# Where the sums for seven half products are made: from the second layer's first block into its second

## The chip, the cores and the metric

The kernel runs on one core of a Trainium2 chip. That core has TensorE (PE: matmuls, with its weight loads listed as PEld), VectorE (DVE), ScalarE (ACT), GpSimd (POOL) and SyncE (SP), which here only starts DMAs. The engines run beside each other; each takes its own instructions strictly in the order of the program and waits on semaphores for the others. The metric is the time of one execution on the device, in microseconds (us); lower is better.

## The reference

Three stages, one after another, all in float32: a linear attention with decay, then a layer with a rational function, then a layer with a cosine. The change lies in the last one.

```python
# attention: state = alpha[t] * state + outer(k[t], v[t]); y[t] = q[t] @ state     (4 x 8 heads, 768 steps, 48 wide)
# first layer, 3072 tokens, 384 -> 2048 -> 384
h = x @ w_in
P = a[0] + a[1] * h + a[2] * h**2 + a[3] * h**3
Q = 1.0 + abs(b[0]) * abs(h) + abs(b[1]) * h**2
x = (P / (Q + 1e-06)) @ w_out
# second layer, the same sizes, weights of its own
h = x @ w_in
out = (h * cos(h)) @ w_out
```

## The kernel before

**Tiles.** Tokens are columns: 3072 tokens are six blocks of 512 (`NC` = 6, `TB` = 512; `HT` = 256 is half a block). The hidden width 2048 is 16 chunks `f` of 128 (`NF`), the model width 384 is three of 128 (`NK`). A step `n` is one chunk of one block; `layers(n)` (line 797 on) issues one step, and `where(n)` tells layer `m`, block `blk` and chunk `f`. In the second layer (m = 1, n from 96 on) f runs fastest, then the block.

**Precision.** A float32 product is made of three matmuls in the type fp32r: each operand is split into a rounded part ("hi") and the rest ("lo"), and hi x hi, hi x lo and lo x hi are added up (`PASSES`). So a plain step has nine matmuls of 128x512 for h (`gemm1`, L640) and nine for the output (`gemm2`, L656). `gemm2` of a step is issued some steps later, by `lag`: 4 steps for a plain chunk, 5 for one by seven.

**Between the products** (`cosine`): L78 (ACT) and L79 (DVE) reduce the angle, L742 (ACT) takes the sine, L744 (DVE) makes g = h cos h, L686 (ACT) rounds it to hi, and L691 (POOL) makes its lo. hi and lo have three buffers each, g four, z three.

**Weights of the second layer.** They arrive as 64-bit words and are converted by hand, one weight at a time (`tick`, three operations a step here): L67 and L68 on ACT, L72 and L73 on DVE. In the next step `w_hi` rounds (L187, ACT) and `w_lo` makes the rest (L196, POOL). The second layer's output weights are converted during the layer's first block, each about one step before `gemm2` reads it; the last one is done in the second block's third step. Their raw words pass through two buffers named raw, which `seven_out0` also uses for its q.

**Seven half products.** From the second block on (`by_seven`), two neighbouring chunks (a pair, j = f // 2) are multiplied by a scheme that replaces eight products of half a block by seven, at the price of sums. `seven(n, 0)` and `seven(n, 1)` each write the one bank r0 (L566); ACT copies it out at L602 and L608; POOL combines at L603, L614 and L616; DVE adds to h at L625. `seven(n, 2)` makes what is left of both chunks. The scheme needs sums of the weights, once for each pair (`weights_sums(j)`: DVE L516 twice and L520 to L523, ACT L525 twice, POOL L526 twice), and sums of the columns of x, once for each block (`x_sums0`: DVE L533, L537, L538; `x_sums1`: ACT L557 and DVE L558, three of each). `weights_sums` writes one of its results over the first 128 columns of the pair's odd weight, which a plain product of that chunk still needs (for the last pair a tile of its own takes it).

**What sets the order.** The order is written out by hand in `layers`: `gemm1`, `cosine`, `w_hi`, the split of the next block's x (`x_hi`, L785, ACT), `gemm2`, `seven(n, 1)`, `weights_sums`, `x_sums0`, the next block's x loads (f = 8), `x_lo` (L789, DVE, f = 11 to 13), `x_sums1`, then the fetch of weights, `tick` and `w_lo`. In the first block of the second layer `weights_sums` runs in each of the steps f = 8 to 15, one pair a step; `x_sums0` runs at f = 10 and `x_sums1` at f = 14, for the block to come.

Of the kernel before, what the change touches and what calls it, by code (L numbers as in the profile page):

```python
# [10 lines left out]
F32R = mybir.dt.float32r  # L11
# [3 lines left out]
ALU = mybir.AluOpType  # L15
# [3 lines left out]
NC, C = 6, 128  # L19
HP = 4  # L20
NF = DFF // 128
NK = DM // 128
TB = B * C
# [16 lines left out]
def attn_then_two_moe(ctx, tc, kqT, aT, vP, w1i, w1o, ma, mb, w2i, w2o, out):  # L40
    nc = tc.nc
# [40 lines left out]
    const = main.enter_context(tc.tile_pool(name="const", bufs=1))  # L82
# [8 lines left out]
    def temp(tag, dtype=F32, shape=(128, TB)):  # L91

        bufs = {"z": 3, "ah": 2, "g": 4, "hi": 3, "lo": 3}[tag]
        return el.tile(list(shape), dtype, tag=tag, name=tag, bufs=bufs)
# [369 lines left out]
    def where(n):  # L464
        m, r = divmod(n, N1)
        if n < 2 * H1:
            return 0, *divmod(n, H1)
        if n < 2 * NF:
            blk, f = divmod(n - 2 * H1, NF - H1)
            return 0, blk, H1 + f  # L470
        return m, *divmod(r, NF)
# [8 lines left out]
    HT = TB // 2  # L480
    PASSES = ((0, 0), (0, 1), (1, 0))
    s_in = {}
    x_t = {}
    held = {}

    def by_seven(n):

        m, blk, f = where(n)
        return m == 1 and 0 < blk and (blk < NC - 1 or f < NF - 2)

    def lag(n):

# [6 lines left out]

    def weights_sums(j):  # L500

        if j == 0:
            held["kq"] = const.tile([128, 5 * 2 * HP * C], F32R, tag="kq", name="s_in")
            held["s1"] = [const.tile([128, 128], F32R, tag=f"s{i}", name=f"s1_{i}") for i in range(2)]
        if j < 6:
            flat = held["kq"][:, 2 * DM * j:2 * DM * (j + 1)].rearrange("p (a b c) -> p a b c", a=2, b=3)
            s = [flat[:, i] for i in range(2)]
        else:
            s = [
                const.tile([128, 3, 128], F32R, tag=f"v{2 * (j - 6) + i}", name=f"s_in{j}{i}") for i in range(2)  # L510
            ]
        first = held["s1"] if j == NF // 2 - 1 else [ws[0][2 * j + 1][:, i, 0:128] for i in range(2)]
        a = temp("z", shape=(128, 4, 128))
        for i in range(2):
            w = ws[0][2 * j + i].bitcast(F32)
            nc.vector.tensor_tensor(  # L516
                out=a[:, 2 * i:2 * i + 2].rearrange("p a b -> p (a b)"), in0=w[:, 0, 0:256], in1=w[:, 1, 0:256], op=ALU.add
            )
        t = temp("g", shape=(128, 4, 128))
        nc.vector.tensor_tensor(out=t[:, 0], in0=a[:, 2], in1=a[:, 3], op=ALU.add)  # L520
        nc.vector.tensor_tensor(out=t[:, 1], in0=t[:, 0], in1=a[:, 0], op=ALU.subtract)
        nc.vector.tensor_tensor(out=t[:, 2], in0=a[:, 0], in1=a[:, 2], op=ALU.subtract)
        nc.vector.tensor_tensor(out=t[:, 3], in0=a[:, 1], in1=t[:, 1], op=ALU.subtract)  # L523
        for hi, lo, of in ((first[0], first[1], t[:, 0]), (s[0], s[1], t[:, 1:])):
            nc.scalar.activation(out=hi, in_=of, func=AF.Copy)  # L525
            nc.gpsimd.tensor_tensor(out=lo, in0=of, in1=hi.bitcast(F32), op=ALU.subtract)  # L526
        s_in[j] = [[first[i]] + [s[i][:, k] for k in range(3)] for i in range(2)]

    def x_sums0(blk):

        raw = xt[1, blk][:, 1].bitcast(F32)
        t = [in_p.tile([128, TB], F32, tag="p", name="t") for _ in range(2)]
        nc.vector.tensor_tensor(  # L533
            out=t[0].rearrange("p (a b) -> p a b", a=2), in0=raw[:, 0:2, HT:],
            in1=raw[:, 0].rearrange("p (a b) -> p a b", a=2), op=ALU.subtract,
        )
        nc.vector.tensor_tensor(out=t[1][:, :HT], in0=raw[:, 1, HT:], in1=t[0][:, :HT], op=ALU.subtract)  # L537
        nc.vector.tensor_tensor(out=t[1][:, HT:], in0=raw[:, 1, :HT], in1=t[1][:, :HT], op=ALU.subtract)  # L538
        held["t"] = t

    def x_sums1(blk):

        t = held.pop("t")
        tag, words = (("st", 4 * DM), ("a", 3 * HP * (C + 1)))[blk % 2]
        to = const.tile([128, words], F32R, tag=tag, name=f"x_t{blk}")[:, :6 * HT].rearrange(
            "p (a b c) -> p a b c", a=2, b=3
        )
        if blk < NC - 1:
            first = [xt[1, blk][:, i, 0, HT:] for i in range(2)]
        else:  # L550
            first = [held["kq"][:, 12 * DM + HT * i:12 * DM + HT * (i + 1)] for i in range(2)]
        x_t[blk] = [[first[i]] + [to[:, i, k] for k in range(3)] for i in range(2)]
        for hi, lo, of in (
            (first[0], first[1], t[0][:, :HT]), (to[:, 0, 0], to[:, 1, 0], t[0][:, HT:]),
            (to[:, 0, 1:], to[:, 1, 1:], t[1].rearrange("p (a b) -> p a b", a=2)),
        ):
            nc.scalar.activation(out=hi, in_=of, func=AF.Copy)  # L557
            nc.vector.tensor_tensor(out=lo, in0=of, in1=hi.bitcast(F32), op=ALU.subtract)  # L558
# [85 lines left out]
    def gemm2(n):  # L644
        m, blk, f = where(n)
        d = T.pop(n)
        assert m or (0, 1, f) in ready
        first = f == 0 or in_parts(m, blk) and f == H1
        last = f == NF - 1 or in_parts(m, blk) and f == H1 - 1
        for k in range(NK):  # L650
            if first:
                acc_out()
                acc[k] = ps_acc.tile([128, TB], F32, tag=f"acc{k}", name=f"acc{k}")
            ks = slice(k * 128, (k + 1) * 128)
            for i, (w, g) in enumerate(((0, "hi"), (0, "lo"), (1, "hi"))):
                nc.tensor.matmul(  # L656
                    acc[k], ws[1][f][:, w, ks], d[g], start=first and i == 0, stop=last and i == 2
                )
            if last:
                outs.append((m, blk, f, k))  # L660
# [117 lines left out]

    def x_cols(m, blk, kk):

        return slice(0, HT if m and 0 < blk < NC - 1 and kk == 0 else TB)

    def x_hi(m, blk, kk):
        x, cs = xt[m, blk], x_cols(m, blk, kk)
# [16 lines left out]
    def all_ok1():  # L801
        cnt = bank("r1", (1, 2 * NU))
        nc.tensor.matmul(cnt, ones, ok.rearrange("p a b -> p (a b)"), start=True, stop=True)
        tot = const.tile([1, 1], F32, name="tot")
        nc.vector.tensor_reduce(tot, cnt, mybir.AxisListType.X, ALU.add)
        nc.vector.tensor_scalar(bad, tot, 128.0 * 2 * NU - 0.5, None, ALU.is_lt)


    def layers(n):
        slot[0] = n + LEAD  # L810
        if n == N1 + 4:
            gemm2(N1 - 1)
            done[0] += 1
        if n < 2 * N1:
            gemm1(n)
        if n == NF:
            all_ok0()
        if n == NF + 2:
            all_ok1()
        m, r = divmod(n, N1)  # L820
        blk, f = divmod(r, NF)
        nxt = (m, blk + 1) if blk + 1 < NC else (m + 1, 0)
        at, load = f - 11, f == 8
        if n < NF:
            nxt, at, load = (0, 1), n - 5, n == 3
        elif n < 2 * NF:
            at, load = f - 12, f == 10
        split = 0 <= at < NK and n < 2 * N1 and nxt[0] < 2
        rational(n)
        cosine(n)  # L830
        w_hi()
        if split:
            x_hi(*nxt, at)
        second(n)
        if n < 2 * N1 and by_seven(n) and n % 2 == 0:
            seven(n, 1)
            seven_out1(n)
        if m == 1 and blk == 0 and f >= NF // 2:
            weights_sums(f - NF // 2)
        if m == 1 and nxt[0] == 1 and f == 10:  # L840
            x_sums0(nxt[1])
        if n < 2 * N1 and nxt[0] < 2 and load:
            for kk in range(NK):
                x_load(*nxt, kk)
        if split:
            x_lo(*nxt, at)
        if m == 1 and nxt[0] == 1 and f == 14:
            x_sums1(nxt[1])
        i = n - (N1 - NF)
        if n < 2 * NF:  # L850
            if n > 1:
                w_fetch(2 * NF)
                tick(1 if n > 2 else 0, 1)
        elif n < N1 - NF:
            w_fetch(3 * NF + NO)
            if not split:
                tick(1, 1)
        elif n < N1:
            w_fetch(4 * NF)
            if i > 3:  # L860
                tick(1, 1)
        else:
            w_fetch(4 * NF)
            tick(3 if n > N1 + 3 else 1, 1)
        if 0 <= i < NF:
            w_load(i)
        if 0 <= i - 6 < NO:
            w_load(NF + i - 6)
        w_lo([nc.gpsimd])
# [7 lines left out]
    with tc.manual_schedule():  # L877
# [16 lines left out]
        for n in range(-3, NU + 1):  # L894
# [21 lines left out]
            kk = (n - 12) // 2 if n in (12, 14, 16) else None  # L916
# [201 lines left out]
```

## Time and profile before

| | us |
|---|---|
| median of 3 runs (lowest to highest) | 963.41 (962.22 to 965.50) |
| the profiled execution | 964.45 |
| its span, first to last instruction | 962.7 |
| PE busy | 910.3 (95%) |
| DVE busy | 745.5 (77%) |
| ACT busy | 699.6 (73%) |
| POOL busy | 732.0 (76%) |

The rows below come from that one execution; times in them are us from the start of its span. The page splits the span into 40 slices of 24.07 us, with a digit for the busy share of each engine in tenths (9 is 90% or more). A busy share says nothing of who waits for whom: that is in the timeline of an engine, where a bracket behind a row gives how long the engine was idle before it and whose end released it, and in the chain of waits, which follows the work that ended last back from instruction to instruction. PEclk is the granted clock of TensorE, 1.00 being its upper level of 2.4 GHz.

### The profile page before, as it was taken

The numbers are of one execution on the slowest core, as the hardware profiler recorded it, in microseconds if no ns is written. First come the engines' busy times: TensorE is split into PE (matmuls) and PEld (weight loads), VectorE is DVE, ScalarE is ACT, GpSimd is POOL, SyncE is SP. The second block draws the span as 40 slices with busy tenths as digits, with TensorE's granted clock in tenths as the row PEclk, the third lists the DMA queues.
The fourth block names the chain that finished last, engine by engine and source line by source line (L and its number), as shares of the span: only waits on it lengthen the run. The fifth ranks groups of instructions, "written<-read, shape, count | busy, mean of one in ns | idle before, by whom it ended". The sixth has DMA issues, their size and how long they took to land.

```text
span 962.7 us, 15405 instructions
## 1 busy us (share of the span) xinstructions
PE 910.3 (95%) x5327; PEld 751.1 (78%) x5327; DVE 745.5 (77%) x1226; ACT 699.6 (73%) x1280; POOL 732.0 (76%) x693
## 2 busy tenths in 40 slices
PE   7797899999999999999999996699999999999996
PEld 6676777778888888888888874578888888888885
DVE  8988879999999989989799578656647658466451
ACT  6899987879878888788788766566666666666662
POOL 5898998989889888989799555566666666666662
PEclk9999999999999999999999999799999999999999
DMA  8999831101122131141364231120010020200001
GB/s 276 323 313 327 285 116 33 33 17 34 66 82 83 50 115 34 65 132 34 115 205 140 82 115 49 34 83 1 1 66 1 1 66 1 66 1 1 33 1 37
DMA packets 47030, 84.69 MB, mean 88 GB/s; under 512 B 5504, under 2 KB 22144, under 8 KB 46944
## 3 DMA queue, kind: packets, MB, share of 16 engines
q1 hardware_dynamic: 46944, 83.62, 26.5%
q8 instruction: 44, 0.72, 0.3%
q14 instruction: 42, 0.34, 0.1%
HBM read 63.15 MB, written 20.45 MB: 87 GB/s over the span
## 4 chain that ended last, share of the span: by engine, by line
PE 71%; DVE 10%; DMA 7%; ACT 6%; issue 3%; POOL 2%; SPq 1%; DVEq 0%; ACTq 0%; POOLq 0%
PE acc L656 36%; PE b L640 19%; PE r L566 8%; PE b L566 8%; DMA spare<-w1i 2%; DMA x<-x0d 2%; DMA a<-aT 2%; DVE z L516 1%; DMA x0d<-g 1%; DVE g L744 1%; DVE st L72 1%; ACT st L67 1%; ACT hi L686 1%; DVE g L722 1%; POOL w L196 1%
## 5 line engine op out<-in xcount | busy, mean ns | idle before, releaser
L656 PE MATMUL acc<-hi,w 128*128 128x512 f32 x1152 | 394.1, 397 | 19.3 <-POOL w L196 18.2
L691 POOL TENSOR_TENSOR lo<-g,hi 128x512 fp32r<-128x512 f32 x192 | 256.9, 1338 | 98.3 <-ACT hi L686 91.9
L656 PEld LDWEIGHTS acc<-hi,w 128*128 128x128 f32 x1152 | 216.5, 189 | 70.5 <-POOL w L196 21.9
L640 PE MATMUL b<-x,w 128*128 128x512 f32 x1026 | 261.3, 399 | 0.7 <-DVE g L709 0.6
L640 PEld LDWEIGHTS b<-x,w 128*128 128x128 f32 x1026 | 194.3, 190 | 49.8 <-DVE g L709 2.1
L656 PE MATMUL acc<-lo,w 128*128 128x512 f32 x576 | 228.5, 397 | 0.0
L686 ACT ACTIVATE hi<-g 128x512 fp32r<-128x512 f32 x192 | 121.4, 632 | 93.8 <-DVE g L722 51.8
L717 POOL TENSOR_TENSOR z<-z,ah 128x512 f32<-128x512 f32 x96 | 127.3, 1326 | 8.0
L656 PEld LDWEIGHTS acc<-lo,w 128*128 128x128 f32 x576 | 108.5, 188 | 22.9
L744 DVE TENSOR_TENSOR g<-ah,b 128x512 f32<-128x512 f32 x76 | 51.8, 682 | 71.8 <-ACT ah L742 71.8
L79 DVE SCALAR_TENSOR_TENSOR ah<-z,b 128x512 f32<-128x512 int32 x76 | 52.0, 685 | 46.9 <-ACT z L78 46.8
L718 DVE TENSOR_TENSOR g<-g,b 128x512 f32<-128x512 f32 x96 | 65.3, 680 | 24.8 <-ACT g L715 24.2
L716 POOL TENSOR_SCALAR z<-ah,cq 128x512 f32<-128x512 f32 x96 | 75.3, 785 | 1.0 <-ACT ah L714 0.9
L715 ACT ACTIVATE g<-b,cq 128x512 f32<-128x512 f32 x96 | 74.6, 777 | 0.0
L722 DVE SCALAR_TENSOR_TENSOR g<-g,cq,r 128x512 f32<-128x512 f32 x96 | 70.9, 738 | 0.1
L709 DVE SCALAR_TENSOR_TENSOR g<-g,cq,b 128x512 f32<-128x512 f32 x96 | 70.7, 736 | 0.0
L603 POOL TENSOR_TENSOR q<-q 128x256 f32<-128x256 f32 x39 | 28.8, 738 | 53.2 <-ACT q L602 53.2
L742 ACT ACTIVATE ah<-ah,half_pi 128x512 f32<-128x512 f32 x96 | 68.8, 717 | 0.2 <-DVE ah L79 0.2
L726 ACT ACTIVATE r<-z,lnb 128x512 f32<-128x512 f32 x96 | 66.7, 695 | 1.8 <-POOL z L717 1.6
L711 DVE SCALAR_TENSOR_TENSOR r<-z,r 128x512 f32<-128x512 f32 x96 | 65.6, 684 | 0.0
L706 DVE SCALAR_TENSOR_TENSOR z<-z,r 128x512 f32<-128x512 f32 x96 | 65.0, 677 | 0.0
L566 PE MATMUL b<-x,w 128*128 128x256 f32 (+1 forms) x291 | 64.3, 351 | 0.0
(154 smaller groups left out, 1646.5 us busy)
## 6 DMA issues: line engine op xcount, KB each, us to landing
kq<-kqT SPq DMA_DIRECT2D x24, 512.0 KB, 5.4
raw<-w2i SPq DMA_DIRECT2D x16, 384.0 KB, 3.0
w<-wd SPq DMA_DIRECT2D x16, 384.0 KB, 3.0
raw<-w2o SPq DMA_DIRECT2D x16, 384.0 KB, 3.0
v<-vP SPq DMA_DIRECT2D x24, 192.0 KB, 5.0
x<-x0d SPq DMA_DIRECT2D x18, 256.0 KB, 3.5
x1d<-o SPq DMA_DIRECT2D x18, 256.0 KB, 2.1
x<-x1d SPq DMA_DIRECT2D x18, 256.0 KB, 3.6
```

Of the source, the lines that this page charges most:

```text
L566: nc.tensor.matmul(out[:, cs], a[w], b[xx], start=first, stop=True, skip_group_check=True)
L640: nc.tensor.matmul(h, ws[0][f][:, w, ks], x[:, xx, kk, :], start=i == 0, stop=i == 8)
L656: nc.tensor.matmul(acc[k], ws[1][f][:, w, ks], d[g], start=first and i == 0, stop=last and i == 2)
L686: nc.scalar.activation(out=t["hi"], in_=t["g"], func=AF.Copy)
L691: eng.tensor_tensor(out=t["lo"], in0=t["g"], in1=t["hi"].bitcast(F32), op=ALU.subtract)
L709: nc.vector.scalar_tensor_tensor(g, g, cq[:, 3:4], two["h"], ALU.add, ALU.mult)
L715: nc.scalar.activation(out=g, in_=h, func=AF.Identity, scale=cq[:, 5:6], bias=cq[:, 4:5])
L716: nc.gpsimd.tensor_scalar(zz, ah, cq[:, 1:2], cq[:, 0:1], ALU.mult, ALU.add)
L717: nc.gpsimd.tensor_tensor(out=zz, in0=zz, in1=ah, op=ALU.mult)
L722: nc.vector.scalar_tensor_tensor(g, g, cq[:, 2:3], r, ALU.add, ALU.mult)
L726: nc.scalar.activation(out=r, in_=two["z"], func=AF.Ln, scale=LN_S, bias=lnb)
L742: nc.scalar.activation(out=t["r"], in_=t["r"], func=AF.Sin, bias=half_pi)
```

## The change

- The first two pairs of the second layer's second block (blk = 1, f = 0 to 3) become plain steps; `by_seven` takes them out.
- `weights_sums` no longer runs in block 0 (f = 8 to 15). It runs in block 1, at odd f: at f = 1 for pair 2, at f = 3 for pair 3, and so on to pair 7 at f = 11, then pairs 0 and 1 at f = 13 and 15 for the blocks after it.
- For block 1, `x_sums0` (still at block 0's f = 10) runs on POOL instead of DVE, and `x_sums1` runs at block 1's f = 0 instead of block 0's f = 14. As block 1's first chunks are plain, its x is split over the whole block's width, and its first sum goes into the tile kq, as the last block's does.

```diff
--- before.py
+++ after.py
@@ -486,7 +486,7 @@
     def by_seven(n):
 
         m, blk, f = where(n)
-        return m == 1 and 0 < blk and (blk < NC - 1 or f < NF - 2)
+        return m == 1 and 0 < blk and (blk > 1 or f >= 4) and (blk < NC - 1 or f < NF - 2)
 
     def lag(n):
 
@@ -499,8 +499,7 @@
 
     def weights_sums(j):
 
-        if j == 0:
-            held["kq"] = const.tile([128, 5 * 2 * HP * C], F32R, tag="kq", name="s_in")
+        if j == 2:
             held["s1"] = [const.tile([128, 128], F32R, tag=f"s{i}", name=f"s1_{i}") for i in range(2)]
         if j < 6:
             flat = held["kq"][:, 2 * DM * j:2 * DM * (j + 1)].rearrange("p (a b c) -> p a b c", a=2, b=3)
@@ -530,22 +529,25 @@
 
         raw = xt[1, blk][:, 1].bitcast(F32)
         t = [in_p.tile([128, TB], F32, tag="p", name="t") for _ in range(2)]
-        nc.vector.tensor_tensor(
+        eng = nc.gpsimd if blk == 1 else nc.vector
+        eng.tensor_tensor(
             out=t[0].rearrange("p (a b) -> p a b", a=2), in0=raw[:, 0:2, HT:],
             in1=raw[:, 0].rearrange("p (a b) -> p a b", a=2), op=ALU.subtract,
         )
-        nc.vector.tensor_tensor(out=t[1][:, :HT], in0=raw[:, 1, HT:], in1=t[0][:, :HT], op=ALU.subtract)
-        nc.vector.tensor_tensor(out=t[1][:, HT:], in0=raw[:, 1, :HT], in1=t[1][:, :HT], op=ALU.subtract)
+        eng.tensor_tensor(out=t[1][:, :HT], in0=raw[:, 1, HT:], in1=t[0][:, :HT], op=ALU.subtract)
+        eng.tensor_tensor(out=t[1][:, HT:], in0=raw[:, 1, :HT], in1=t[1][:, :HT], op=ALU.subtract)
         held["t"] = t
 
     def x_sums1(blk):
 
         t = held.pop("t")
+        if blk == 1:
+            held["kq"] = const.tile([128, 5 * 2 * HP * C], F32R, tag="kq", name="s_in")
         tag, words = (("st", 4 * DM), ("a", 3 * HP * (C + 1)))[blk % 2]
         to = const.tile([128, words], F32R, tag=tag, name=f"x_t{blk}")[:, :6 * HT].rearrange(
             "p (a b c) -> p a b c", a=2, b=3
         )
-        if blk < NC - 1:
+        if 1 < blk < NC - 1:
             first = [xt[1, blk][:, i, 0, HT:] for i in range(2)]
         else:
             first = [held["kq"][:, 12 * DM + HT * i:12 * DM + HT * (i + 1)] for i in range(2)]
@@ -778,7 +780,7 @@
 
     def x_cols(m, blk, kk):
 
-        return slice(0, HT if m and 0 < blk < NC - 1 and kk == 0 else TB)
+        return slice(0, HT if m and 1 < blk < NC - 1 and kk == 0 else TB)
 
     def x_hi(m, blk, kk):
         x, cs = xt[m, blk], x_cols(m, blk, kk)
@@ -835,8 +837,8 @@
         if n < 2 * N1 and by_seven(n) and n % 2 == 0:
             seven(n, 1)
             seven_out1(n)
-        if m == 1 and blk == 0 and f >= NF // 2:
-            weights_sums(f - NF // 2)
+        if m == 1 and blk == 1 and f % 2:
+            weights_sums((f + 3) // 2 % (NF // 2))
         if m == 1 and nxt[0] == 1 and f == 10:
             x_sums0(nxt[1])
         if n < 2 * N1 and nxt[0] < 2 and load:
@@ -844,7 +846,9 @@
                 x_load(*nxt, kk)
         if split:
             x_lo(*nxt, at)
-        if m == 1 and nxt[0] == 1 and f == 14:
+        if m == 1 and nxt == (1, 2) and f == 0:
+            x_sums1(1)
+        if m == 1 and nxt[0] == 1 and nxt[1] > 1 and f == 14:
             x_sums1(nxt[1])
         i = n - (N1 - NF)
         if n < 2 * NF:
```

## Rows read from the trace of the kernel before

**Rows 1.** The page's forty slices: PE's busy share of each, in tenths.

```profile
PE   7797899999999999999999996699999999999996
```

**Rows 2.** Busy time in stretches: us, then PE, PEld, DVE, ACT, POOL; PEclk, DMA share, GB/s.

```profile
575.50:590.74 15.24, 9.46 (x38) 6.68 (x37) 14.00 (x25) 8.34 (x18) 8.29 (x9) 0.98 0.16 54
...
590.74:611.29 20.55, 16.20 (x55) 12.04 (x54) 17.73 (x32) 12.36 (x27) 10.92 (x12) 0.85 0.14 47
...
645.21:685.50 40.29, 40.29 (x227) 34.94 (x227) 26.38 (x37) 24.18 (x44) 25.93 (x25) 1.00 0.00 1
```

**Rows 3.** PE's timeline around the change: start, us, line, what ended the wait.

```profile
556.20 2.26 PE L640 MATMUL b<-x,w 128*128 128x512 f32 x9
...
560.40 2.26 PE L640 MATMUL b<-x,w 128*128 128x512 f32 x9
...
573.77 0.73 PE L656 MATMUL acc<-hi,w 128*128 128x512 f32 x2 [2.20 <-POOL w L196]
```

**Rows 4.** Chain of waits, 556 to 574 us: start, us, engine, written tile, line.

```profile
556.44 0.69 DVE g L744
...
560.24 0.66 DVE g L744
...
566.93 0.68 DVE g L744
...
573.60 0.68 DVE g L744
```

**Rows 5.** PE's timeline in the third block: where two pairs in a row begin.

```profile
701.47 0.52 PE L566 MATMUL r<-x_t,s_in 128*128 128x256 f32 x3
...
709.53 0.52 PE L566 MATMUL r<-x_t,s_in 128*128 128x256 f32 x3
```

**Rows 6.** ACT's timeline in block 0: a rounded g that waits for PE.

```profile
582.68 0.63 ACT L686 ACTIVATE hi<-g 128x512 fp32r<-128x512 f32 x1 [2.37 <-PE acc L656]
```

**Rows 7.** An x_sums0 operation of DVE beside one of POOL, both timelines, block 1.

```profile
663.80 1.80 DVE L533 TENSOR_TENSOR t<-x 128x512 f32<-128x512 f32 x1
...
663.76 1.29 POOL L691 TENSOR_TENSOR lo<-g,hi 128x512 fp32r<-128x512 f32 x1 [0.27 <-ACT hi L686]
```

**Rows 8.** DVE's busy time: x_sums0 and x_sums1 (tile t), and the rests (L789).

```profile
663.00:667.00 4.00, 3.07 (x3) 1.00 0.02 4
...
681.00:685.00 4.00, 2.87 (x3) 1.00 0.00 0
...
656.00:690.00 34.00, 4.10 (x3) 1.00 0.00 1
```

**Rows 9.** One set of sums in block 0: DVE's timeline; busy times of L525, L526.

```profile
568.13 1.86 DVE L516 TENSOR_TENSOR z<-w 128x256 f32<-128x256 f32 x2
...
570.83 0.28 DVE L523 TENSOR_TENSOR g<-z,g 128x128 f32<-128x128 f32 x1
...
567.00:573.20 6.20, 0.84 (x2) 1.00 0.22 63
...
567.00:573.20 6.20, 1.64 (x2) 1.00 0.22 63
```

**Rows 10.** DVE's and POOL's timelines in a pair of the third block.

```profile
714.57 0.69 DVE L744 TENSOR_TENSOR g<-ah,b 128x512 f32<-128x512 f32 x1 [2.31 <-ACT ah L742]
...
715.17 0.68 DVE L79 SCALAR_TENSOR_TENSOR ah<-z,r 128x512 f32<-128x512 int32 x1
...
715.77 0.69 DVE L625 TENSOR_TENSOR b<-b,q 128x512 f32<-128x512 f32 x1
...
714.88 1.31 POOL L616 TENSOR_TENSOR g<-q,z 128x512 f32<-128x512 f32 x1
```

**Rows 11.** ACT's timeline there: the half products' copies and what follows.

```profile
702.38 0.60 ACT L602 ACTIVATE q<-r 128x512 f32<-128x512 f32 x1 [1.89 <-PE r L566]
...
713.32 0.60 ACT L608 ACTIVATE z<-r 128x512 f32<-128x512 f32 x1 [1.27 <-PE r L566]
...
713.82 0.71 ACT L742 ACTIVATE ah<-ah,half_pi 128x512 f32<-128x512 f32 x1
```

## The prediction

> **What bounds the kernel now.** I read the page's forty slices first: TensorE (PE) is at nine tenths or more from the middle of the first layer to the end, with one hole, at slices 25 and 26 [rows 1]. The table of stretches then shows what fills it. In the second half of the second layer's first block PE is busy for 9.46 of 15.24 us, while VectorE (DVE) is for 14.00 of them, and for 17.73 of the next 20.55. In 590.74 to 611.29 the granted clock is 0.85, so part of PE's busy time there is slow matmuls. In the second half of the next block PE is busy for all of 40.29 us at clock 1.00 and DVE for 26.38 of it [rows 2]. So DVE holds the end back in the first block's second half, and PE holds it afterwards.
>
> PE's timeline puts the border where `weights_sums` begins. The plain steps f = 7 and 8 start 4.20 us apart, which is PE's own work (18 matmuls of 0.233 us); from f = 10 on PE waits for POOL's L196, the rest of a converted output weight, 2.20 us in the step after [rows 3]. The chain of waits says why L196 is late: before f = 8 one round from L744 to L744 (L744, L686, L187, L67, L68, L742) takes 3.80 us, below PE's 4.20; with the sums in it, 6.67 us [rows 4]. DVE's L516 to L523 stand in front of L72 and L73, and ACT's two L525 in front of L67 and L68.
>
> **What the stretch costs now.** A pair of steps by seven half products takes 8.06 us, read in the third block, where PE never waits [rows 5]. Block 2 starts two pairs before 701.47, at 685.35. From 560.40 (f = 8) that is 124.95 us. PE's work in it at full clock is 8 x 4.20 = 33.6 plus 8 x 8.06 = 64.5, less one output product of 2.1 (the lag grows from 4 steps to 5 once): 96.0 us. So 29.0 us of the stretch are waits and slow clock. That is the most that the change can give back, less what it adds.
>
> **The change part by part.**
> *Two pairs made plain.* A plain pair is 8.40 us, one by seven 8.06: 2 x 0.34 = 0.7 us more on PE, nothing hides it.
>
> *The sums leave block 0.* Steps f = 8 to 15 fall back to the round of 3.80 us, so PE sets them at 4.20. At f = 8 the weight's rest ends at 560.24 (the next L744 starts on it, [rows 4]), and PE reads it at 560.40 + 2.1 = 562.5: a lead of 2.2 us, which grows by 0.40 a step until the three buffers of hi stop it (L686 then waits for PE, [rows 6]); I take 3.0.
>
> *Block 1's x sums go to POOL (f = 10) and their second half to block 1's f = 0.* No row has `x_sums0` on POOL. The bounds are 2.6 us (1.29 for 512 columns twice, [rows 7]) and 3.07 (DVE's own time, [rows 8]). They stand before L196 in POOL's queue and eat 2.6 to 3.1 of a lead of 3.0 in that one step: taken as nothing, 0.3 us at worst. The x rests at f = 11 to 13 stay on DVE, 4.10 / 3 = 1.37 us each [rows 8]; some 0.4 of that falls into DVE's waits, which makes the round about 4.8 us, three times 0.6 over PE. f = 14 and 15 give 0.8 back. At f = 0 `x_sums1` puts 2.87 us into DVE's queue ahead of L72 [rows 8]; about 0.8 of it falls into a wait, round 6.05 with ACT's part, 1.85 over. At f = 1 the first sums (pair 2) meet the last weight's conversion, a step of 6.67 [rows 4], 2.47 over. Sum 1.8 - 0.8 + 1.85 + 2.47 = 5.3, less the lead of 3.0: PE waits 2.3 us at f = 2 (0 if the rows overlap better, 5 if there is no lead). No DMA is moved: w2o is fetched in the same steps, and the raw buffers have no q in them before f = 4.
>
> *The sums in block 1.* Now six pairs have one set of sums each. Work of one set: DVE 2.98 us from L516's start at 568.13 to L523's end at 571.11 (two L516, then four of 128x128); ACT 0.84; POOL 1.64 [rows 9]. DVE's own work in a pair is six operations at 0.60 spacing [rows 10] = 3.6, so 6.6 of 8.06 with the sums. POOL is at 25.93 / 5 = 5.2 a pair [rows 2] + 1.64 = 6.8. By busy time it fits. By order it doesn't quite. PE's second half product (`which` 1) needs bank r0 back from L602, and L608 waits for that product: ACT now waits for PE at both [rows 11], 1.9 and 1.3 us of slack. With the sums there is a round that passes through both: L608, +0.5 L742, +0.75 L744, +0.6 L79, +0.6 L625 [rows 10, 11], +0.6 sums, 3.1 to the end of L523, +0.05 the second L525, +0.4 L742 of the next step, +0.6 L602 done 0.6 later, then the product 0.7 and L608: 8.55; through L742, L744 and L686 it is 8.65. I take 8.65, 0.6 over a pair. Below it 8.06 is possible (the slack of 1.9 us hides it for three pairs); above it, see the rule below.
>
> The first of the six (f = 4) has one elementwise step less, since the lags overlap, and keeps 8.06. In three of them block 2's x is prepared as well, DVE 3.07 + 1.37, 2 x 1.37 and 2.87 = 10.05 us [rows 8]. DVE has 8.65 - 6.6 = 2.05 free in a round, 6.15 in three. So it costs between 3.9 (all the free time is used) and 10.05 (none). Going through the queues in order, `x_sums0` finds 0.85 free, the rests at f = 12 and 13 nearly all they need, `x_sums1` 1.0: 5.4. That is nearer the low end, as in block 1 of before the same work cost PE nothing [rows 2].
>
> Sum from f = 4 to block 2: 8.06 + 5 x 8.65 + 5.4 = 56.7 us. PE's own work there is 6 x 8.06 - 2.1 = 46.3 (the missing output product is now at f = 8). PE is late by 10.4 us.
>
> *Sum.* 29.0 - 0.7 - 2.3 - 10.4 = 15.6 us gained. The profiled execution took 964.45 us (span 962.7 and 1.75 around it), so 948.9, taken as 949; it lies 1.0 us above the median of the three runs, so against the median 948 would do.
>
> **A rule that speaks against it.** DVE's L533 starts at 663.80, 0.04 us after a POOL L691 of 1.29, and takes 1.80; it ends 0.55 after POOL's end [rows 7]. The two L516 take 1.86 for two of 128x256 [rows 9], against 0.55 for L533's 128x512 after POOL's end. So a DVE operation with both inputs in SBUF stands still while POOL works, while L744 and L625, with one input in PSUM, keep 0.69 beside L616 [rows 10]. In block 1 POOL's L616 and L691 follow each other, and the sums start in the middle of the first: L516 can lose to both, 0.7 us more a round, five times: 3.5 us, 952.5.
> The Trainium skill, "SBUF — State Buffer", section "Who interferes with whom", states it as an exclusive lock: a VectorE instruction with two SBUF inputs and a GpSimd one that reads SBUF block each other for the whole instruction, and whichever starts first wins. The trace agrees at L533 (1.80 us).
>
> **The rivals.**
> *Hidden in block 1.* ACT's slack at L602 and L608 takes the rounds up, and the x work uses all the free time: PE late by 2.7 (the gap at f = 8 that the missing product leaves) to 5 us in block 1 and 0 to 1 at f = 2. Gain 22.3 to 25.6: 939 to 942; for it: before, x preparation cost nothing there. Against: POOL and DVE are both over eight tenths.
> *Heavier.* The lock as above, none of DVE's free time used (4.6 more), and some matmuls at half clock in the pairs at f = 10 to 15, as in 590.74 to 611.29 [rows 2]: 957 to 961. Against the clock: PE would be busy some 75% there, against 62% in the stretch before it fell.
> *Not the sums.* If the conversion itself, not the sums, held block 0, nothing would be gained: 964. Against: the same conversion runs at 4.20 a step before f = 8 [rows 3].
> *Slower.* DVE and POOL take turns altogether in block 1: 6.6 + 6.8 = 13.4 us a pair, and 5.4 for x: 85.8 against 46.3, 39.5 us late; with 2.3 and 0.7 against 29.0 that is 13.5 us slower, 978. It decides from a mean of 12.5 us a pair on ((46.3 + 29.0 - 0.7 - 2.3 + 2.9) / 6). Against: L744, L625 and L79 don't slow beside POOL [rows 10].
>
> **How the numbers follow.** The forecast, 942 to 957 with 949 in it (with the lock 952.5): 0.65. Hidden: 0.17. Heavier: 0.09. Not the sums: 0.04. Slower: 0.05. The range 938 to 959 leaves out the very end of hidden, half of heavier and the last two, 0.2 in all. A measurement of this kernel tells 0.3% (2.9 us) from no change; faster by more than that has 0.91, the same 0.04, slower 0.05.
>
> **What would show it.** In the profile after: steps f = 8 to 15 of block 0 at 4.20 us with no wait for L196 and clock 1.00; a wait of some 2 us for L196 at block 1's f = 2; in block 1 PE waiting for L602, most at f = 8 and from f = 10 on, pairs of 8.6 to 11.8 us, 8.06 again from block 2 on. The prediction is wrong if block 1's pairs stay at 8.06 (then 941 or less), if they pass 10 us all along (then 957 or more), or if block 0's second half still waits.

## The result and the profile after

The changed kernel takes 953.77 us (median of four, 951.43 to 956.72) against 964.41 before: ratio 0.9894, 95% interval 0.9854 to 0.9934. The forecast was 949 with a range of 938 to 959 and 0.91 on faster. So the way and the range were right; the gain is 10.6 us where 15.6 were forecast. Every reading of a trace below comes from one profiled execution of its kernel.

The profiled execution took 956.72 us, its span 955.0. I compare one stretch throughout, as it holds all that the change touches: from the first block's f = 8 (second layer) to f = 2 of the third block, which is where PE waits for the last time. Before, that is 560.40 to 693.41, 133.0 us ([rows 3]; [rows 5] less one pair). After, it is 563.36 to 687.77, 124.4 us: 8.6 us gained. The prediction's sum gives 117.4.

The rest of the profiled difference lies outside. The changed kernel reaches f = 8 later by 3.0 us, before anything that the change touches. TensorE's clock is lower there between 10 and 20 us; in the traces of the kernels below, whose code is the same up to there, it is 0.50 to 1.00 in these 10 us, so this differs from one execution to the next. That it accounts for all of the 3.0 us isn't shown. The four times of the changed kernel fall into two pairs, 951 to 952 with a mean clock of 0.989 and 956 to 957 with 0.98. From f = 2 of the third block to the end it needs 2.1 us less, all of it behind PE's last matmul, which starts 260.6 us after that point in both. 8.6 - 3.0 + 2.1 = 7.7, the difference of the spans. First the stretch from 10 us on before, then after (us, then busy times of PE, PEld, DVE, ACT, POOL; PEclk, DMA share, GB/s):

```profile
10.00:20.00 10.00, 8.84 (x101) 7.78 (x103) 9.07 (x23) 6.94 (x14) 6.76 (x8) 0.84 0.83 257
```

```profile
10.00:20.00 10.00, 9.83 (x72) 8.50 (x72) 9.17 (x24) 6.19 (x12) 6.12 (x7) 0.50 0.92 278
```

The page's slices of the changed kernel answer to [rows 1]: the hole of two sixes has become a shallow dent of eights, and the clock is still short of full in one slice.

```profile
PE   8797899999999999999999999888899999999997
...
PEclk7999999999999999999999999899999999999999
```

The stretches of the changed kernel show what the dent is made of. The columns are those of [rows 2]: us, then busy times of PE, PEld, DVE, ACT, POOL; PEclk, DMA share, GB/s.

```profile
563.36:605.36 42.00, 42.00 (x182) 33.84 (x181) 29.15 (x44) 29.91 (x60) 24.75 (x21) 1.00 0.30 94
605.36:620.23 14.87, 11.12 (x37) 8.55 (x36) 10.93 (x20) 7.94 (x16) 9.24 (x9) 0.77 0.00 0
620.23:636.35 16.12, 16.12 (x92) 13.97 (x90) 10.17 (x17) 8.68 (x16) 11.38 (x12) 1.00 0.28 99
636.35:646.77 10.42, 7.79 (x38) 6.69 (x36) 8.18 (x18) 5.57 (x11) 6.96 (x8) 0.84 0.00 0
646.77:654.84 8.07, 8.07 (x46) 7.00 (x45) 7.12 (x10) 4.32 (x8) 5.95 (x6) 1.00 0.01 2
654.84:667.14 12.30, 9.88 (x47) 8.24 (x46) 11.53 (x20) 7.14 (x15) 8.80 (x8) 0.86 0.00 0
667.14:675.20 8.06, 8.06 (x47) 6.99 (x46) 6.78 (x11) 5.82 (x12) 6.07 (x6) 1.00 0.00 1
675.20:687.77 12.57, 9.85 (x47) 8.24 (x45) 9.07 (x17) 6.58 (x12) 8.17 (x8) 0.86 0.01 1
```

The first row is ten plain steps at 4.20 us with PE busy throughout: block 0's second half no longer holds PE at all. Then four places lose time, each with a clock below 1.00: f = 2 and 3 of block 1 (14.87 us for 8.40 of work), f = 8 and 9 (10.42 for 5.96, as one output product falls away there), f = 12 and 13 (12.30 for 8.06), and f = 0 and 1 of the third block (12.57 for 8.06). PE's timeline names the wait in each; the bracket is the idle time before, and what ended it:

```profile
611.83 1.22 PE L658 MATMUL acc<-hi,w 128*128 128x512 f32 x2 [3.75 <-POOL w L196]
...
639.85 0.62 PE L568 MATMUL r<-s_in,w 128*128 128x256 f32 x3 [2.63 <-ACT q L604]
...
660.23 0.62 PE L568 MATMUL r<-s_in,w 128*128 128x256 f32 x3 [2.42 <-ACT q L604]
...
680.88 0.62 PE L568 MATMUL r<-x,w 128*128 128x256 f32 x3 [2.72 <-ACT q L604]
```

The line numbers have moved by two (L604 and L610 were L602 and L608, L746 was L744). The places are those that the prediction named; their sizes aren't quite.

**Where the wait at f = 2 comes from.** DVE's timeline of the changed kernel, from f = 10 to f = 2. The distance from one L746 to the next is the round of a step, 3.80 us when nothing is added [rows 4]:

```profile
570.79 0.68 DVE L746 TENSOR_TENSOR g<-ah,b 128x512 f32<-128x512 f32 x1
...
574.99 0.68 DVE L746 TENSOR_TENSOR g<-ah,b 128x512 f32<-128x512 f32 x1
...
577.86 1.84 DVE L791 TENSOR_TENSOR x<-x 128x512 fp32r<-128x512 f32 x1 [1.59 <-POOL t L538]
...
580.68 0.68 DVE L746 TENSOR_TENSOR g<-ah,b 128x512 f32<-128x512 f32 x1
...
592.11 1.44 DVE L72 SCALAR_TENSOR_TENSOR st<-st,raw 128x384 int32<-128x384 int32 x1 [1.49 <-ACT raw L68]
...
594.05 0.68 DVE L746 TENSOR_TENSOR g<-ah,b 128x512 f32<-128x512 f32 x1
...
598.77 0.68 DVE L746 TENSOR_TENSOR g<-ah,b 128x512 f32<-128x512 f32 x1
...
604.61 0.68 DVE L746 TENSOR_TENSOR g<-ah,b 128x512 f32<-128x512 f32 x1
...
612.12 0.67 DVE L746 TENSOR_TENSOR g<-ah,b 128x512 f32<-128x512 f32 x1
```

The round is 5.69 us behind `x_sums0` (574.99 to 580.68), 4.33 at f = 12 and again at f = 13; 4.72 at f = 15 (594.05 to 598.77), where L72 takes 1.44 us; 5.84 at f = 0, with `x_sums1`; 7.51 at f = 1, with the first weights' sums. It is never below 4.20 from f = 11 on, so the lead only shrinks, and PE runs into it at f = 2. Two of these rounds need the other engines' rows beside them, from ACT's, POOL's and DVE's timelines:

```profile
577.15 0.62 ACT L787 ACTIVATE x<-x 128x512 fp32r<-128x512 f32 x1
...
577.85 1.30 POOL L693 TENSOR_TENSOR lo<-g,hi 128x512 fp32r<-128x512 f32 x1
...
583.13 0.90 DVE L791 TENSOR_TENSOR x<-x 128x512 fp32r<-128x512 f32 x1 [1.18 <-issue]
...
592.12 1.01 POOL L196 TENSOR_TENSOR w<-st,w 128x384 fp32r<-128x384 f32 x1
...
603.55 0.54 DVE L72 SCALAR_TENSOR_TENSOR st<-st,raw 128x384 int32<-128x384 int32 x1
```

At f = 11 the bracket of the x rest L791 names POOL's L538, but that ended at 576.91 (576.17 + 0.74); what ends at 577.77, just before L791 starts, is ACT's L787, as in the steps after. What is longer is L791 itself: 1.84 us, where it takes 0.90 at f = 12 and 0.96 at f = 13. It stands beside all of POOL's L693 (577.85 to 579.15) and ends 0.55 us after it. L693's input, the hi of L688, was there at 576.83; `x_sums0` and L196 in POOL's queue held L693 back by 1.0 us, onto L791. The other 0.4 us by which this round is longer than f = 12's is ACT's L688 (at 576.20) waiting for PE, where the lead is still at its full. So the differences on POOL cost DVE time though DVE doesn't wait for them. At f = 14 and 15 L72 has both inputs in SBUF and starts with POOL's L196 beside it (592.11 and 592.12): 1.44 us. With the same inputs and no POOL operation beside it, at f = 0, it takes 0.54.

**Where the waits in block 1 come from.** ACT's timeline of the changed kernel: L610, the copy of the second half product out of r0, once a pair.

```profile
624.00 0.60 ACT L610 ACTIVATE z<-r 128x512 f32<-128x512 f32 x1 [0.86 <-PE r L568]
...
632.07 0.60 ACT L610 ACTIVATE z<-r 128x512 f32<-128x512 f32 x1 [0.90 <-POOL q L605]
...
640.92 0.60 ACT L610 ACTIVATE z<-r 128x512 f32<-128x512 f32 x1
...
650.55 0.60 ACT L610 ACTIVATE z<-r 128x512 f32<-128x512 f32 x1 [0.58 <-PE r L568]
...
661.59 0.60 ACT L610 ACTIVATE z<-r 128x512 f32<-128x512 f32 x1
...
670.91 0.60 ACT L610 ACTIVATE z<-r 128x512 f32<-128x512 f32 x1 [0.36 <-PE r L568]
...
681.94 0.60 ACT L610 ACTIVATE z<-r 128x512 f32<-128x512 f32 x1
```

Distances 8.07, 8.85, 9.63, 11.04, 9.32 and 11.03: 57.9 us for six pairs, where the prediction's round made 56.7.

### The profile page after: what moved, and what is told of

It is laid out like the page before. It is cut to its first block, busy times and chain, and to the rows that moved or that the text cites. A ratio compares the mean times of both kernels' runs of the same rounds, so it can differ in the third digit from the quotient of the medians.

```text
span 955.0 us, 15338 instructions
## 1 busy us (share of the span) xinstructions
PE 914.6 (96%) x5309; PEld 755.8 (79%) x5309; DVE 742.3 (78%) x1219; ACT 696.4 (73%) x1276; POOL 730.6 (77%) x690
## 5 line engine op out<-in xcount | busy, mean ns | idle before, releaser
L693 POOL TENSOR_TENSOR lo<-g,hi 128x512 fp32r<-128x512 f32 x192 | 257.5, 1341 | 102.6 <-ACT hi L688 96.2
L642 PE MATMUL b<-x,w 128*128 128x512 f32 x1053 | 266.5, 398 | 0.6 <-DVE g L711 0.5
L642 PEld LDWEIGHTS b<-x,w 128*128 128x128 f32 x1053 | 198.2, 189 | 50.0 <-DVE g L711 2.1
L688 ACT ACTIVATE hi<-g 128x512 fp32r<-128x512 f32 x192 | 121.3, 632 | 98.9 <-DVE g L724 51.5
L746 DVE TENSOR_TENSOR g<-ah,b 128x512 f32<-128x512 f32 x76 | 51.9, 682 | 70.2 <-ACT ah L744 67.8
L744 ACT ACTIVATE ah<-ah,half_pi 128x512 f32<-128x512 f32 x96 | 68.7, 716 | 0.0
L716 ACT ACTIVATE ah<-b 128x512 f32<-128x512 f32 x96 | 56.5, 588 | 7.5 <-PE b L642 7.1
L568 PE MATMUL b<-x,w 128*128 128x256 f32 (+1 forms) x276 | 61.8, 355 | 0.0
```

The costliest lines, as they stand in the source:

```text
L568: nc.tensor.matmul(out[:, cs], a[w], b[xx], start=first, stop=True, skip_group_check=True)
L642: nc.tensor.matmul(h, ws[0][f][:, w, ks], x[:, xx, kk, :], start=i == 0, stop=i == 8)
L688: nc.scalar.activation(out=t["hi"], in_=t["g"], func=AF.Copy)
L693: eng.tensor_tensor(out=t["lo"], in0=t["g"], in1=t["hi"].bitcast(F32), op=ALU.subtract)
L744: nc.scalar.activation(out=t["r"], in_=t["r"], func=AF.Sin, bias=half_pi)
```

## The experiments

Each starts from the changed kernel and changes what its diff shows; "..." marks lines left out. "The stretch" is the one above. A time with a range is the median of four or more executions, one without is of a single one; the row "before" has the nine executions taken beside experiments 3 and 6. The single times of experiments 1 to 3 lie inside the changed kernel's own range and decide nothing: what is compared there are waits and rounds. In experiments 5 and 6 the output product that falls away as the lag grows lies behind the stretch, so their stretches hold 2.1 us more of PE's work.

| kernel | time, us | stretch, us |
|---|---|---|
| before | 965.1 (961.7 to 966.9) | 133.0 |
| changed | 953.8 (951.4 to 956.7) | 124.4 |
| 1. `x_sums1` at f = 14 again | 956.5 | 123.8 |
| 2. `x_sums0` on DVE again | 951.6 | 121.6 |
| 3. words in a PSUM bank | 951.8 | 118.7 |
| 4. sums in even steps | 947.9 (947.2 to 951.6) | 118.8 |
| 5. block 1 plain | 944.1 (942.1 to 947.9) | 113.0 |
| 6. block 1 plain, sums spread | 940.1 (938.0 to 940.6) | 108.9 |

**1. The second half of the x sums back in block 0.**

```diff
-        if m == 1 and nxt == (1, 2) and f == 0:
-            x_sums1(1)
-        if m == 1 and nxt[0] == 1 and nxt[1] > 1 and f == 14:
+        if m == 1 and nxt[0] == 1 and f == 14:
             x_sums1(nxt[1])
```

> The changed kernel with one part undone: the second half of the second block's x sums is back at the first block's f = 14, ahead of f = 0 of the second block. Read from the trace: PE's wait for the last output weights' rest at the second block's f = 2, 3.75 us in the changed kernel. Theory A (the lead that the elementwise round has over PE is used up step by step from f = 11 on, and never comes back, since the round is above 4.20 us in all of these steps): the place doesn't matter, the sum of the rounds is the same, the wait stays at 3.75 +- 0.7 us. Theory C (the wait comes from the x sums' second half standing one step ahead of the first weights' sums): the wait falls by the 1.6 us that this step's round is over PE, to about 2 us. Time: 952 to 957 by A, 949 to 953 by C.

PE's timeline and the stretch from f = 2 to f = 4 (columns as above):

```profile
611.89 0.73 PE L658 MATMUL acc<-hi,w 128*128 128x512 f32 x2 [2.98 <-POOL w L196]
```

```profile
606.18:617.82 11.64, 8.66 (x37) 6.69 (x36) 8.70 (x14) 5.96 (x12) 7.75 (x7) 1.00 0.00 0
```

2.98 us, just below what A expects and well above C's 2; 0.3 us more are lost a step earlier. So moving the x sums' second half ahead by two steps saves half a microsecond, not 1.6. PE still waits. What changes more is the clock: 1.00 here against 0.77, so f = 2 and 3 take 11.64 us instead of 14.87. The stretch as a whole is only 0.6 us shorter, since block 1 then waits longer (69.9 us from f = 4 to the end of the stretch, where the changed kernel has 67.5).

**2. The x sums' first half back on DVE.**

```diff
-        eng = nc.gpsimd if blk == 1 else nc.vector
+        eng = nc.vector
```

> The changed kernel with one part undone: the second block's first x sums run on DVE, not on POOL. In the changed kernel the round from L746 to L746 grows to 5.69 us in the step behind them, since the x rest on DVE waits 1.6 us for POOL. Theory A (a step's excess counts wherever it sits, and DVE's 3.07 us in the step f = 10 add about 1.6 to the round, as they did in the kernel before, 8.31 against 6.67): the wait at f = 2 stays at 3.75 +- 0.7 us and the time at 952 to 957. Theory D (POOL took the sums off the elementwise round for nothing, as the prediction had it): on DVE the wait grows by 2 to 3 us, to about 6, and the time by 3 to 4 us.

DVE's timeline at f = 10 and 11, then PE's wait, then f = 2 to f = 4:

```profile
568.43 0.68 DVE L746 TENSOR_TENSOR g<-ah,b 128x512 f32<-128x512 f32 x1
...
570.81 1.41 DVE L538 TENSOR_TENSOR t<-x,t 128x256 f32<-128x256 f32 x1
...
573.19 0.68 DVE L746 TENSOR_TENSOR g<-ah,b 128x512 f32<-128x512 f32 x1
```

```profile
608.22 0.73 PE L658 MATMUL acc<-hi,w 128*128 128x512 f32 x2 [2.51 <-POOL w L196]
```

```profile
602.99:615.71 12.72, 10.21 (x38) 7.86 (x36) 9.68 (x18) 6.47 (x15) 8.47 (x8) 0.87 0.00 0
```

Neither expectation holds: the wait falls, from 3.75 to 2.51 us. On DVE the three differences make a round of 4.76 us (568.43 to 573.19), 0.96 above an empty one, since most of them fall into the 1.5 us that DVE waits for ACT's L68 in each step. On POOL they made one of 5.69 in the next step, since they push L693 onto the x rest. The rounds of f = 10 to 13 add up to 17.8 us here and to 18.6 in the changed kernel: 0.8 of the 1.2 us by which the wait falls; the other 0.4 comes from shorter rounds at f = 14 and 1. So the part of the change that took work off DVE cost 0.8 to 1.2 us of waiting, by one execution of each.

**3. The last conversions' words in a PSUM bank.**

```diff
             return bank(f"r{w[2] % 2}", (128, TB), I32)[:, :DM]
+        if N1 + NF - 2 <= slot[0] - LEAD < N1 + NF + 2:
+            return bank("r0", (128, TB), I32)[:, :DM]
         return None
```

> The changed kernel, with the conversion's words in PSUM bank r0 for the last four steps that convert (f = 14 and 15 of the second layer's first block, f = 0 and 1 of the second) instead of SBUF; r0 is free there until f = 4. In the changed kernel L72 then has two inputs in SBUF and takes 1.44 us beside POOL's L196 at f = 14 and 15, against 0.56 before, and the round from L746 to L746 is 4.72 us instead of about 4.2. Theory A (that slower L72 uses up lead, 0.5 us in each of two steps, and some in the next two): L72 takes 0.56, the wait at f = 2 falls from 3.75 to 1.8 to 2.8 us. Theory F (DVE has slack there, and the wait comes from f = 0 and 1 alone): the wait stays within 0.4 us of 3.75. Time by A 949 to 954 (less if TensorE's clock doesn't fall behind the wait), by F 951 to 957.

DVE's L72 at f = 14 and 15, PE's wait, f = 2 to f = 4:

```profile
592.92 0.56 DVE L72 SCALAR_TENSOR_TENSOR r<-st,r 128x384 int32<-128x384 int32 x1 [1.44 <-ACT r L68]
...
596.72 0.56 DVE L72 SCALAR_TENSOR_TENSOR r<-st,r 128x384 int32<-128x384 int32 x1 [1.45 <-ACT r L68]
```

```profile
610.50 0.73 PE L660 MATMUL acc<-hi,w 128*128 128x512 f32 x2 [1.56 <-POOL w L198]
```

```profile
606.22:616.44 10.22, 8.66 (x38) 6.69 (x36) 7.23 (x15) 5.64 (x12) 6.38 (x7) 1.00 0.00 0
```

A holds, a little beyond its figure: L72 is back at 0.56 us, the wait falls by 2.2 us to 1.56, and the clock stays at 1.00. The stretch is 5.7 us shorter, 4.65 of it at f = 2 and 3.

**4. The same sums, one step over.**

```diff
-        if m == 1 and blk == 1 and f % 2:
-            weights_sums((f + 3) // 2 % (NF // 2))
+        if m == 1 and blk == 1 and (f == 3 or f > 3 and f % 2 == 0):
+            weights_sums(2 if f == 3 else (f + 2) // 2 % (NF // 2))
+        if m == 1 and blk == 2 and f == 0:
+            weights_sums(1)
```

> The changed kernel with the weights' sums of block 1 in even steps instead of odd ones: pair 2 at f = 3, then pairs 3 to 7 at f = 4, 6, 8, 10, 12, pair 0 at f = 14 and pair 1 at the third block's f = 0. The same work, but on DVE it stands in front of the odd step's L746, where DVE idles 2.3 us or more in an undisturbed pair, and not between two L627, where it doesn't idle. Theory A (the order of the round that goes through bank r0's two copies on ACT makes the waits in block 1): that round shrinks from 8.65 to about 7 us, below PE's 8.06. PE's waits for L604, in the changed kernel 2.63, 2.42 and 2.72 us, fall to 3 us or less in all (the x work stays), and the wait at f = 2 to 1.5 or less, since the first sums no longer meet the last conversion. From the first block's f = 8 to the third block's f = 2, 124.4 us in the changed kernel, 113 to 118; time 942 to 948. Theory B (DVE and POOL together are too full in block 1, whatever the order): the waits for L604 stay at 7 us or more in all, only the one at f = 2 shrinks; time 948 to 953.

Who PE waited for in this kernel between 598 and 680 us (total, times, longest):

```profile
PE r L568 <- DVE x_t L560: 2.4, 1, 2.4
PE r L568 <- ACT q L604: 1.7, 2, 1.0
PE r L568 <- ACT s_in L524: 1.6, 1, 1.6
PE r L568 <- POOL s_in L525: 1.5, 3, 0.7
PE r L568 <- ACT x_t L559: 0.9, 1, 0.9
PE acc L658 <- POOL w L196: 0.5, 1, 0.5
```

A holds for what it is about: PE's waits for L604 fall from 7.8 us to 1.7, and the wait for L196 from 3.75 to 0.5. B expected 7 or more for L604. One set of the eight leaves the block here, from f = 15 to the third block's f = 0, so the wait at that place isn't a clean comparison; those at f = 8 and f = 12, which lie before it, fall from 2.63 and 2.42 us to 0.75 and 0.99 with as many sets in the block up to there. The stretch, 118.8 us, is a little above A's 113 to 118, as this order brings waits of its own that I hadn't counted: the sums of a pair are now finished just as the pair begins (L524 and L525, 3.1 us), and the third block's x sums stand behind a set of weights' sums at f = 14 (L559 and L560, 3.3 us). In all PE still waits 8.6 us, where the changed kernel has 11.5.

**5. Block 1 plain.**

```diff
-        return m == 1 and 0 < blk and (blk > 1 or f >= 4) and (blk < NC - 1 or f < NF - 2)
+        return m == 1 and 1 < blk and (blk < NC - 1 or f < NF - 2)
...
-        if m == 1 and blk == 1 and f % 2:
-            weights_sums((f + 3) // 2 % (NF // 2))
-        if m == 1 and nxt[0] == 1 and f == 10:
+        if m == 1 and blk == 1 and f in (2, 4, 6, 8, 9, 11, 13, 15):
+            weights_sums(((2, 4, 6, 8, 9, 11, 13, 15).index(f) - 1) % (NF // 2))
+        if m == 1 and nxt[0] == 1 and nxt[1] > 1 and f == 10:
...
-        if m == 1 and nxt == (1, 2) and f == 0:
-            x_sums1(1)
```

> The whole second block plain, seven half products from the third block on. No x sums for the second block; the weights' sums in the second block at f = 2 (pair 7), 4, 6, 8, 9, 11, 13, 15 (pairs 0 to 6). PE's own work grows by six pairs of 0.34 us, 2.1 us in all. In plain steps no product waits for a copy out of bank r0, and DVE, ACT and POOL have no half products to combine. Theory A: no wait of PE from the second block's f = 3 on, the wait at f = 2 under 1 us (two of its sources are gone), the clock 1.00 throughout; from the first block's f = 8 to the third block's f = 2 109 to 111 us against 124.4; time 939 to 944. Theory B (throughput of DVE and POOL): PE still waits 4 us or more in the second block, from f = 8 on where the x work and the sums meet; time 944 to 950.

PE's waits between 598 and 690 us:

```profile
PE r L567 <- ACT q L603: 3.1, 2, 2.0
PE acc L657 <- POOL w L196: 1.6, 1, 1.6
```

A holds from f = 4 on, one step later than it says: PE's steps are 4.20 us without a wait, though all eight sets of sums are made in the block. At its ends the kernel still waits, 1.64 us for the last weight's rest at f = 3, with the first sums in front of that rest at f = 2, and 2.00 us at the third block's f = 0, behind the x sums at f = 14 and the sums at f = 13 and 15 (1.07 more at its f = 4, beyond the stretch). So 113.0 us instead of 109 to 111; the ratio to before is 0.9795 (0.9738 to 0.9852).

**6. Block 1 plain, the sums spread, the words in a bank.**

```diff
-        if m == 1 and blk == 1 and f in (2, 4, 6, 8, 9, 11, 13, 15):
-            weights_sums(((2, 4, 6, 8, 9, 11, 13, 15).index(f) - 1) % (NF // 2))
+        when = {(1, 3): 7, (1, 5): 0, (1, 7): 1, (1, 9): 2, (1, 11): 3, (1, 13): 4, (2, 4): 5, (2, 8): 6}
+        if m == 1 and (blk, f) in when:
+            weights_sums(when[blk, f])
```

(on the kernel of experiment 5, with the diff of experiment 3)

> The second block plain, as in the run before of that kind, with three things moved: the first weights' sums (pair 7) from f = 2 to f = 3, behind the last conversion; the others at f = 5, 7, 9, 11, 13 (pairs 0 to 4) and in the third block at f = 4 and 8 (pairs 5 and 6), so that f = 14 and 15 hold the x sums alone; and the last conversions' words in bank r0. In the run before of that kind PE waited 1.64 us for the last weight's rest at the second block's f = 3 and 2.00 us for a copy out of r0 at the third block's f = 0. Theory A (each of these waits comes from work that stands in the same or the step before): both vanish or fall under 0.5 us, one pair's sums alone in the third block cost 0.6 us at most, from the first block's f = 8 to the third block's f = 2 109 to 110.5 us, time 939 to 943. Theory B (the elementwise engines are too full for the sums anywhere behind the conversion): the waits move into the third block, 2 us or more in all at f = 4 to 10, time 943 to 947.

PE's waits between 590 and 700 us, then the stretch:

```profile
PE r L569 <- ACT q L605: 1.1, 1, 1.1
```

```profile
561.49:670.34 108.85, 108.85 (x479) 88.21 (x477) 70.42 (x122) 68.34 (x131) 58.45 (x52) 1.00 0.16 51
```

PE is busy for all of the stretch: 108.85 us, which is 24 plain steps of 4.20 and one pair of 8.06. The one wait left, 1.07 us, is at the third block's f = 4, where an output product falls away as the lag grows; that is above A's 0.6 and below B's 2. Both waits of experiment 5 at the block's ends are gone, as A expects; since the sums and the words were moved together, which of the two removed the wait at f = 3 isn't shown. This kernel takes 940.08 us, 0.974 of before (0.9719 to 0.9761), and beats both kernels. It uses half products in fewer places than the kernel before, and pays 2.7 us of matmuls for that (eight pairs of 0.34) to be rid of the 29.0 us of waits and slow clock in the stretch.

## Why the prediction was right or wrong

- **What bounded the kernel, and that the sums did: right.** Ten steps from f = 8 on run at 4.20 us with no wait (first row of the stretches after, against [rows 2, 3]). "Not the sums" is out.
- **The plain pairs at 0.7 us: right.** Plain steps are 4.20 us in every kernel here, pairs by seven 8.06.
- **`x_sums0` on POOL "taken as nothing": wrong.** I asked only whether L196 behind it on POOL would be late for PE, and not what the late L196 and L693 would stand beside: L693 holds the x rest on DVE, 1.84 us instead of 0.9. The round of that step is 1.5 over PE, and experiment 2 puts the price at 0.8 to 1.2 us of waiting at f = 2. (The expectation of experiment 2 still has the x rest waiting for POOL's differences, by the bracket; ACT's row speaks against it.) The sum for f = 11 to 13, 1.8, came out (1.5 + 0.13 + 0.13) by luck: the rests at f = 12 and 13 cost 0.13 each instead of 0.6, which hid the term that was left out.
- **"f = 14 and 15 give 0.8 back": wrong.** They cost 1.0 (rounds of 4.71 and 4.72 us). The words of the last four conversions (f = 14 to f = 1) aren't in PSUM, in the kernel before neither, so that L72 has two inputs in SBUF, and with the sums gone it starts together with L196. The lock that I wrote down as a rival for L516 acted on L72, which I hadn't looked at; the rows of L72 with and without L196 beside it show it (1.44 and 0.54 us), and experiment 3 its price, 2.2 us of waiting. For the sums themselves the case that I priced at 952.5 did not arise: from the first L515 to L519's start it took 1.6 to 2.1 us in block 1 from f = 3 on, where it took 1.9 to 2.0 before.
- **f = 0: right** (5.84 for 6.05). **f = 1: too low**, 7.51 for 6.67. From f = 10 to 1 the rounds are 7.7 us over PE's 4.20 in all, where I had 5.3; the lead was about 4.0 us (7.7 - 3.75), not 3.0, which hid one more. Together the wait was 3.75 where I had 2.3.
- **The clock left out at f = 2: wrong.** Two steps with a wait of 3.75 took 14.87 us where 8.40 + 3.75 = 12.15: 2.7 us of slow matmuls. I had a falling clock only in the rival "heavier", and there only at f = 10 to 15, with an argument against it that didn't hold: it fell in each of the three places in and behind block 1 too (0.84, 0.86, 0.86). With the wait, this place is 6.5 us instead of 2.3.
- **The round through r0: right, as mechanism and nearly as size.** Six pairs took 57.9 us for 56.7, the waits are at f = 8 and from there on, for L604, and experiment 4 takes most of those at f = 8 and 12 away by order alone. The distribution was off: I expected each pair to be late, and PE waits in every second one. The half clock behind the waits at f = 8 and 12 cost little, since the round and not PE was the bound there: from f = 4 to the end of the stretch experiment 3's kernel needs 66.5 us, the changed one 67.5, at mean clocks of 0.97 and 0.92. Only behind the last wait it was paid, by estimate 1.6 us: the places lost 4.5, 4.2 and 4.5 us, 13.2 in all, and the six rounds are 11.6 over PE's own 46.3. So block 1 lost 13.2 us where I had 10.4.
- **The sum.** 29.0 - 0.7 - 6.5 - 13.2 = 8.6 instead of 15.6. Of the 7.0 us that are missing, 4.2 are f = 2, its wait and its clock, and 2.8 are block 1, 1.2 the round and 1.6 the last slow matmuls.
- **The rivals.** "Hidden" would have had block 1 at 8.06 us a pair; "slower" 12.5 or more; the mean round was 9.7.

## What to carry to other kernels

A step that isn't late can still be too full: add up, step by step, what the round of the elementwise engines is above or below the matmul time, and treat the lead as an account that only steps with a shorter round pay into. When work is moved to an idle engine, ask what it pushes back in that engine's queue, and what that then runs beside: here a POOL operation that came 1.0 us late held a DVE operation for 0.9 us. Check a bracket's releaser against the end of its row: here the one named had ended 0.95 us before. And where a matmul bank has a single buffer, put extra work where the engine idles in that bank's round (here the even steps), or take the block out of that scheme for as long as the extra work lasts: experiments 4 and 6 gained 6 and 14 us on the changed kernel with the same eight sets of weights' sums (experiment 6 with plain chunks and the words in a bank besides).

## What the runs showed of the hardware that I had not expected

The granted clock behind a wait of PE doesn't go by the wait's length alone. At the same place, f = 2 of block 1, it fell behind waits of 3.75 us (mean 0.77 over the two steps) and 2.51 us (0.87), and stayed at 1.00 behind 2.98 and 1.56 us. At the third block's f = 0 it fell behind 2.72 us (0.86, changed kernel) and stayed at 1.00 behind 2.96 us (experiment 3). What decides between them stays open here; in this kernel a wait of 2 to 4 us has to be priced both with the clock's fall (1.8 to 2.7 us more, by the four places of the changed kernel and experiment 2's) and without.

VectorE's L72 on 128x384 took 0.56 us with one input in PSUM, 1.44 us with both in SBUF and POOL's L196 started at the same moment, and 0.54 with both in SBUF and no POOL operation beside it. And a 128x128 sum (L519) took 1.20 us at f = 1 of the changed kernel, beside a POOL L693, where it takes 0.29 in the other seven sets. This fits the exclusive lock of the Trainium skill, "SBUF — State Buffer", section "Who interferes with whom": a VectorE instruction with two SBUF inputs stands still while a GpSimd instruction reads SBUF. The trace agrees at L72 (1.44 us against 0.54), and a PSUM bank for one operand was the way out (0.56, experiment 3).
